# Last four k heads gathered by DMA from spare columns, and q/k products moved ahead of the attention phase

## The chip, the cores and the metric

One core of one Trainium2 chip. The metric is the device time of one launch in microseconds (us), median over runs; the profile's span is about 1.7 us shorter than the time. The three batches of experiments ran on three different chips, each beside the kernel before (medians 167.65, 167.1 and 167.67 us), so between batches compare ratios before medians.

## The reference

```python
# S=2048, D=448, H=16 heads of 28; window of 8 positions, dilation 2
xn  = layernorm(x)
qkv = (xn @ wqkv);  q, k, v = split into heads
logits = q . k[pos - 2*j] / sqrt(28),  j = 0..7, masked where pos - 2*j < 0
o   = softmax(logits) @ v[pos - 2*j]
s   = o @ wo
h   = gelu(xn @ w1 + b1) @ w2 + b2           # F = 1792
out = x + s * silu(h)
```

## The kernel before

Even and odd positions are put apart, so that the dilated window is 8 neighbours. A head has 28 columns and takes 32 partitions, so a tile of 128 holds four heads, and q and k need four tiles (g = 0..3) each. The four spare columns per head are unused. D = 448 is 3.5 blocks of 128 rows; two half blocks of 64 rows run side by side on TensorE. Work goes by chunks of 512 positions. In this text, phase 1, 2, 3 is the loop body for c = 0, 1, 2: a first FFN layer (`feed_forward_1`) and five attention units. A last FFN layer and two units follow. In a unit, S are the scores, E their exponentials (times a mask), psO the sums over the values, and o_t is an output tile on its way to DRAM.

```python
psA = tile_pool(bufs=2, PSUM);  psB = tile_pool(bufs=4, PSUM)   # psB is used in turn by all "B" tiles

def qk_pair(c, g, even, copies):        # q and k of 4 heads: 6 full matmuls + 2 of 64 rows
    ...
def v_job(b):                           # 4 matmuls of 448 columns, cast by ACT
    v_put(b, v_mm(b))
def wo_put(t, ps, cs=slice(0, D)):
    ...
    o_t = work.tile([P, D], BF16, name="o_t", tag="o_t", bufs=3)
    nc.vector.tensor_tensor(out=o_t[:, cs], in0=xt(t)[:, cs], in1=sg[:, cs], op=ALU.add)
    nc.sync.dma_start(dram_rows(out_par, t, 1)[:, 0, cs], o_t[:, cs])
def qk_unit(b, after_scores=lambda: None):   # 16 matmuls S = k.q ; exp on ACT ; mask on DVE
    ...
def av_unit(b, E):                           # 16 matmuls psO ; shuffle on DVE ; returns norm()
    ...
for c in range(3):
    feed_forward_1(c, ps, ...)          # with qk_pair(c + 1, 0) inside, output products behind k = 4
    n = c + 1
    qk_pair(n, 1, True, DD)
    for i in range(5):
        if i == 0:
            E = qk_unit(b, lambda: qk_pair(n, 2, ...))
            ...
            qk_pair(n, 3, True, DA)
        else:
            E = qk_unit(b); norm(); ffn2_job(4 * c + i - 1); v_job(next(vs))
            if n + 1 < NC:
                ln_apply(4 * n + 3 + i); ln_dma(4 * n + 3 + i)
        norm = av_unit(b, E)
    norm()
    ps = ffn1(n, 0, True)
```

The softmax here doesn't subtract the row's maximum and nothing guards it: scores larger than these inputs give would overflow.

## Time and profile before

| | before |
|---|---|
| time, median | 167.1 us |
| span of the profiled run | 165.6 us |
| TensorE busy | 158.9 us, 96% |
| VectorE, ACT busy | 68%, 76% |
| small copies on the queue of SyncE (wo) | 16, in 8.16 us |

The lines behind it are in the prediction. Names are PE for TensorE, DVE for VectorE, ACT for ScalarE, POOL for GpSimd, SP for SyncE and SPq for the queue on which SyncE issues DMAs. A timeline line gives start and duration in us, engine, source line, operation, what it writes and reads, and how many instructions are merged; the bracket is idle time before it and what ended it. TensorE has no gaps to speak of: a matmul removed is time removed, as long as nothing else falls behind.

### The profile page before, as it was taken

To read this page: it belongs to the slowest core of one execution; us is meant where nothing else is said; L and a number is where in the kernel's file an instruction comes from. 1 tells how busy PE (TensorE), PEld (TensorE's weight loads), DVE (VectorE), ACT (ScalarE), POOL (GpSimd) and SP (SyncE) were. 2 spreads that over 40 slices of the span, in tenths; PEclk is the share of its full clock that TensorE was granted. 3 is DMA by queue.
4 is the path that set the end of the run, shared out by engine and by line. 5 is a ranking of instruction groups with operands and counts; after the bars stand their busy time and mean duration, and the time that the engine had idled before them with its cause. 6 is when DMAs were issued, how large, how long until landed. Compare 5 with 4: busy or idle time off the path is not lost.

```text
span 165.6 us, 3242 instructions
## 1 busy us (share of the span) xinstructions
PE 158.9 (96%) x1290; PEld 71.8 (43%) x1301; DVE 112.9 (68%) x256; ACT 125.9 (76%) x198; POOL 4.5 (3%) x16
## 2 busy tenths in 40 slices
PE   6899999999999999999999999999999999999990
PEld 2343333345554334445554334335555334445570
DVE  5967890497888638687888308877777507678893
ACT  3773698598887795998887795698888698698830
POOL 7002000000000000000000000000000000000000
PEclk9999999999999999999999999999999999999999
DMA  5999995520111100100211100300000002020011
GB/s 134 302 306 267 325 190 93 164 44 4 32 36 32 32 0 4 55 0 0 36 32 32 36 0 0 112 1 4 0 4 0 0 0 60 31 83 0 4 55 55
DMA packets 15963, 10.62 MB, mean 64 GB/s; under 512 B 7500, under 2 KB 15948, under 8 KB 15948
## 3 DMA queue, kind: packets, MB, share of 16 engines
q1 hardware_dynamic: 15660, 10.18, 24.0%
q10 hardware_dynamic: 288, 0.23, 0.5%
q8 instruction: 10, 0.16, 0.4%
q14 instruction: 5, 0.04, 0.1%
HBM read 7.00 MB, written 1.84 MB: 53 GB/s over the span
## 4 chain that ended last, share of the span: by engine, by line
PE 83%; ACT 7%; DVE 5%; DMA 2%; issue 1%; DVEq 0%
PE ps_y L281 23%; PE ps_h L249 21%; PE ps_qk L197 11%; PE ps_v L228 8%; PE ps_s L331 6%; PE ps_h L258 4%; PE S L355 3%; PE psO L370 3%; ACT hT L264 3%; PE ps_qk L207 3%; DMA x<-in_A_x_dram 2%; ACT th L310 1%; DVE sg L337 1%; DVE st L161 1%; ACT L509 1%
## 5 line engine op out<-in xcount | busy, mean ns | idle before, releaser
L264 ACT ACTIVATE hT<-ps_h,b1f 128x512 bf16<-128x512 f32 x56 | 34.1, 695 | 10.1 <-PE ps_h L258 7.3
L249 PE MATMUL ps_h<-xnT,w 128*128 128x512 bf16 x161 | 39.3, 380 | 0.5 <-issue 0.2
L281 PE MATMUL ps_y<-w,hT 128*128 128x448 bf16 x196 | 39.5, 353 | 0.0
L361 ACT ACTIVATE E<-S 128x976 bf16<-128x976 f32 x34 | 31.6, 983 | 2.1 <-PE S L355 0.8
L281 PEld LDWEIGHTS <-hT 128*128 128x128 bf16 x196 | 18.0, 98 | 16.7
L249 PEld LDWEIGHTS <-w 128*128 128x128 bf16 x168 | 15.0, 98 | 22.1 <-issue 6.4
L363 DVE TENSOR_TENSOR E<-E,mk_gen 128x976 bf16<-128x976 bf16 x30 | 20.0, 666 | 6.7 <-ACT E L361 6.5
L197 PE MATMUL ps_qk<-xnT,wqk 128*128 128x512 bf16 x92 | 22.2, 380 | 0.3 <-issue 0.2
L379 DVE TENSOR_TENSOR oT<-psO,den 128x484 bf16<-128x484 f32 (+1 forms) x17 | 11.3, 662 | 10.1 <-ACT den L378 10.1
L214 DVE CAST qT<-ps_qk 128x512 bf16<-128x512 f32 x16 | 11.0, 687 | 9.5 <-PE ps_qk L207 8.4
L228 PE MATMUL ps_v<-wv,xnT 128*128 128x448 bf16 x68 | 15.7, 353 | 0.1
L311 DVE SCALAR_TENSOR_TENSOR g<-th,y 128x448 bf16<-128x448 bf16 x13 | 7.6, 621 | 10.8 <-ACT th L310 10.8
L337 DVE SCALAR_TENSOR_TENSOR sg<-ps_s,g 128x448 bf16<-128x448 f32 (+2 forms) x17 | 10.1, 592 | 7.0 <-PE ps_s L331 6.9
L233 ACT CAST vw<-ps_v 128x448 bf16<-128x448 f32 x17 | 9.1, 533 | 6.9 <-PE ps_v L228 6.8
L197 PEld LDWEIGHTS <-wqk 128*128 128x128 bf16 x96 | 8.9, 98 | 11.5 <-issue 1.8
L331 PE MATMUL ps_s<-wo,oT 128*128 128x448 bf16 (+2 forms) x68 | 13.4, 342 | 0.0
L377 ACT ACTIVATE den<-den 128x484 f32<-128x484 f32 (+1 forms) x17 | 10.3, 605 | 4.0 <-DVE den L374 4.0
L374 DVE STREAM_SHUFFLE den<-psO 128x484 f32<-128x484 f32 (+1 forms) x17 | 11.7, 695 | 0.0
L378 ACT ACTIVATE den<-den 128x484 f32<-128x484 f32 (+1 forms) x17 | 10.3, 606 | 0.5
L161 DVE BATCH_NORM_STATS2 st<-x 128x6 f32<-128x448 bf16 x16 | 9.8, 610 | 0.9 <-DMA x<-in_A_x_dram 0.8
L331 PEld LDWEIGHTS <-oT 128*128 128x128 bf16 x68 | 6.4, 98 | 5.9 <-issue 0.2
L228 PEld LDWEIGHTS <-xnT 128*128 128x128 bf16 x68 | 6.3, 98 | 6.0 <-ACT xnT L181 0.6
(71 smaller groups left out, 139.8 us busy)
## 6 DMA issues: line engine op xcount, KB each, us to landing
out_dram<-o_t SPq DMA_DIRECT2D x15, 112.0 KB
w<-in_B_w_dram SPq DMA_DIRECT2D x1, 1568.0 KB
x<-in_A_x_dram SPq DMA_DIRECT2D x3, 448.0 KB
w<-in_B_w_dram SPq DMA_DIRECT2D x2, 672.0 KB
wraw<-in_A_wqkv_dram SPq DMA_DIRECT2D x1, 672.0 KB
w<-in_B_w_dram SPq DMA_DIRECT2D x4, 112.0 KB
wo<-in_A_wo_dram SPq DMA_DIRECT2D x16, 24.5 KB
wv<-in_A_wqkv_dram SPq DMA_DIRECT2D x1, 336.0 KB
```

What stands on the lines that cost most here:

```text
L161: nc.vector.bn_stats(out=st[:], in_=xt(t))
L197: nc.tensor.matmul(ps[w][:, :], wqk[:, kt, 16 * w + 4 * g:16 * w + 4 * g + 4, :], xnT[:, kt, LEAD + c * CH:LEAD + (c + 1) * CH], start=(fi ...
L228: nc.tensor.matmul(ps[:, :], xnT[:, kt, o:o + P], wv[:, kt, :], start=(kt == 0), stop=(kt == KT - 1))
L249: nc.tensor.matmul(ps[i][:, :], w1[:, kt, m * P:(m + 1) * P], xnT[:, kt, LEAD + c * CH:LEAD + (c + 1) * CH], start=(first and kt == 0), st ...
L264: nc.scalar.activation(hT[:, m, :], ps[i][:, :], ACT.Gelu_apprx_tanh, bias=b1f[:, m:m + 1])
L281: nc.tensor.matmul(ps[:, :], hT[:, m, tt * P:(tt + 1) * P], w2[:, m, :], start=(m == 0), stop=(m == MT - 1))
L331: nc.tensor.matmul(ps[:, 0:n], oT[:, g, t * P:(t + 1) * P], wo[:, g, cs], start=(g == 0), stop=(g == 3))
L337: nc.vector.scalar_tensor_tensor(out=sg[:, cs], in0=ps[:, 0:cs.stop - cs.start], scalar=0.5, in1=g_sb[t % NG][:, cs], op0=ALU.mult, op1=AL ...
L361: nc.scalar.activation(ev, Sp[p2][:, :, :, 0:QW], ACT.Exp, scale=SCALE)
L363: nc.vector.tensor_tensor(out=ev, in0=ev, in1=mkb, op=ALU.mult)
L374: nc.vector.stream_shuffle(den[:, :, 0:n], psO[:, :, 0:n], [0] * 32)
L379: nc.vector.tensor_tensor(out=oT[:, :, QB * b:QB * b + n], in0=psO[:, :, 0:n], in1=den[:, :, 0:n], op=ALU.mult)
```

## The change

Intent: less work on TensorE. In chunks 1 to 3 the fourth tile of k is no longer a product of its own. Its 112 columns are spread over the spare columns of the other seven q and k tiles (four columns per 32), so that they come out of products made anyway, and 28 small copies per chunk (4 partitions of 1 KB each) bring them to their places in `kT`. q/k products go ahead of the attention units; the values of phases 2 and 3 are made in pairs in the first unit, so that their half blocks run side by side.

```diff
+    def qk_spare(kt):            # fills columns 28..31 of each slot with columns of the last 4 k heads
+        ...
+    def k3_rows(c, g, w):
+        j = 4 * w + g
+        cols = slice(LEAD + c * CH, LEAD + (c + 1) * CH)
+        for h in range(4):
+            nc.sync.dma_start(kT[32 * h + 4 * j:32 * h + 4 * j + 4, 3, cols],
+                              (qT, kT)[w][32 * h + DH:32 * h + 32, g, cols])
     def qk_put(c, g, w, ps, copies):
         copies[w]((qT, kT)[w][:, g, LEAD + c * CH:LEAD + (c + 1) * CH], ps[w][:, :])
+        if c:
+            k3_rows(c, g, w)
+    def q3_job(c, copy):         # q alone for g = 3: 4 matmuls
+        ...
+    def v_pair(b, copy=nc.scalar.copy):   # two value products, 6 full + 2 of 64 rows
+        ...
# feed_forward_1
-            if (c, k) in ((0, 6), (1, 4), (2, 4)):
-                qk_pair(c + 1, 0, True, DD)
+            if c in (1, 2) and k in (2, 3, 4):
+                qk_pair(c + 1, k - 2, False, DD)
+                if k == 3:
+                    q3_job(c + 1, nc.vector.tensor_copy)
-            if k in ((3, 5, 6) if c == 3 else (4,)):
+            if c == 3 and k in (2, 4, 6) or c in (1, 2) and k == 6:
                 ... wo_job
# first attention unit
-                    E = qk_unit(b, lambda: qk_pair(n, 2, False, ...))
+                if i == 0 and c == 0:
+                    E = qk_unit(b, lambda: q3_job(1, nc.vector.tensor_copy))
+                    ln_rstd(8, 4)
+                    qk_pair(1, 1, True, DA)
+                    qk_pair(1, 2, False, DA)
+                    nc.sync.dma_start(x_sb[3][:, :, :], dram_rows(x_par, 12, 4))
+                elif i == 0:
+                    E = qk_unit(b)
+                    if n + 1 < NC:
+                        ln_rstd(4 * n + 4, 4)
+                    v_pair(4 * n)
+                    v_pair(4 * n + 2, nc.vector.tensor_copy)
# later units
-                    v_job(next(vs))
+                    if c == 0 and i in (2, 4):
+                        v_pair(4 * n + i - 2)
```

Cut: start-up order, weight packing, `late_loads` moved behind the last layernorm transpose of phase 1, the order of two output products at the end.

## The prediction

> **What bounds the kernel now.** I read the page first, then the waits of TensorE, then the timeline of all engines around one attention phase, because the change moves work there.
>
> ```profile
> span 165.6 us, 3242 instructions
> ...
> PE 158.9 (96%) x1290; PEld 71.8 (43%) x1301; DVE 112.9 (68%) x256; ACT 125.9 (76%) x198; POOL 4.5 (3%) x16
> ...
> PE 83%; ACT 7%; DVE 5%; DMA 2%; issue 1%; DVEq 0%
> ```
>
> ```profile
> PE ps_w L389 <- DVE wz L98: 1.3, 1, 1.3
> PE pT L177 <- DVE xnb L169: 0.5, 2, 0.2
> ```
>
> TensorE is busy 96% of the span, makes 83% of the chain that ended last, and the waits over 0.2 us in its list (the second fence; us in total, times, longest) are 1.8 us at the start. So a matmul taken out shortens the kernel one for one, unless something then fails to keep up. The timeline of the second attention phase shows how near the others are. Columns are start, duration, instructions.
>
> ```profile
> 69.30 0.67 PE L355 MATMUL S<-qT,kT 28*128 28x122 bf16 x16
> 69.54 1.28 ACT L412 ACT_TABLE_LOAD   x1
> ...
> 77.94 0.40 PE L355 MATMUL S<-qT,kT 28*128 28x122 bf16 x16
> 78.27 2.82 PE L281 MATMUL ps_y<-w,hT 128*128 128x448 bf16 x14
> 78.38 1.86 ACT L361 ACTIVATE E<-S 128x976 bf16<-128x976 f32 x2
> ...
> 80.27 0.67 DVE L363 TENSOR_TENSOR E<-E,mk_gen 128x976 bf16<-128x976 bf16 x1 [0.16 <-ACT E L361]
> 80.76 0.61 ACT L378 ACTIVATE den<-den 128x484 f32<-128x484 f32 x1
> 80.93 0.92 PE L228 MATMUL ps_v<-wv,xnT 128*128 128x448 bf16 x4
> 81.40 0.67 DVE L379 TENSOR_TENSOR oT<-psO,den 128x484 bf16<-128x484 f32 x1 [0.46 <-ACT den L378]
> 81.78 0.40 PE L370 MATMUL psO<-E,vw 128*32 128x122 bf16 x16
> ```
>
> One attention unit is scores S, 14 products of the second FFN layer, 4 value products, then psO. The last mask product ends at 80.94, psO starts at 81.78: 0.84 us of slack, and the value products (0.85 us) are what gives it. Also S at 69.30 took 0.60 us to the next instruction (69.90), where 0.33 is usual: it waited for a late gelu. psO behind it lost 0.20. The same pair is seen in the third phase, so before already loses 2 x 0.47 = 0.94 us that no wait row names.
>
> **What the Trainium skill says.** TensorEngine Tiling (Array Packing), section Key Properties: changing the tiling mode drains TensorE. The trace agrees: 12 full matmuls of 512 columns run from 19.73 to 22.43 (2.70 us), 6 from 17.81 to 19.20 (1.39); six more cost 1.31, so 0.218 each, and 0.08 is left for the switch to 64-row matmuls. From the 448-column ones: 14 take 2.66 (0.190 each), 4 take 0.85 before a switch, leaving 0.09. I use 0.1 us per switch. Perfetto Trace Analysis, section Identifying the Most-Contended Engine, warns that matmul busy time is a poor measure. I therefore take start-to-start times, not the 380 ns mean durations, which overlap. DMA: Bandwidth & Descriptors, section Issuing engines are not separate DMA queues, says issuing costs the sequencer time and the engines are shared; here 16 loads of wo occupy the queue of SyncE from 27.30 for 8.16 us, 0.51 each (median duration 383 ns). Its section on the anatomy of one DMA gives about 2 us of fixed completion time, measured on another issue path; here an output buffer was writable again about 2.1 us after its store, so I use 2.
>
> **The change part by part.**
>
> *q/k products.* In chunks 1 to 3 the fourth pair (7 slots: 6 full and two 64-row matmuls side by side) becomes one q job of 4 full matmuls. 3 x 3 x 0.216 = 1.94 us less on TensorE.
>
> *Value pairs.* Six pairs take 7 slots of 448 columns in place of 8: 6 x 0.19 = 1.14 us less.
>
> *Switches.* Counting mode changes along each phase: the first attention phase gains 2 by its pairs and loses 1 by the missing q/k pair (+1); phases two and three have +2 each, since pairs no longer share borders so well; the last FFN phase puts output products behind k = 2 and 4 between 64-row groups that used to adjoin: +4. Together 9 x 0.1 = 0.9 us more. Net matmul saving 1.94 + 1.14 - 0.9 = **2.2 us**.
>
> *Removed stalls.* The 0.94 us above go away in that form, as the FFN phases get more TensorE work (q/k) for the same gelus.
>
> *Start.* A bias transpose leaves the border before the first q/k pair and weight copies come in fewer instructions: 0.1 us gained. One more warm-up matmul may give it back.
>
> *New stall: units without value products.* In phases two and three units 1 to 4 are S, 14 products, psO: 4.17 - 0.76 = 3.42 us. Counting from the end E of S (78.34): exponentials until E+1.9; logarithm and exponential of the former unit until E+3.03 (80.76+0.61 = 81.37); VectorE takes oT at E+3.06, y at 3.64, the two layernorm instructions at 4.17, shuffle at 4.69, the next unit's two masks from 5.29 to 6.76 (they took 1.47 together at 83.63). psO's tail and the next S need 0.38 + 0.40: so two units cannot take less than 7.54 us where TensorE wants 6.86. Units 2 and 4 of phase two each lose 0.68: 1.36 us. Phase three has no layernorm there; the same chain without its 0.52 gives 7.02, 0.16 over: with its second occurrence 0.25 us. Phase one keeps a value pair in units 2 and 4; unit 3 starts behind their two ACT copies: 0.1 us.
>
> *New stall: first unit of phase two.* Only two output products (1.6 us) stand between the last FFN tile and S. From that tile's end K (67.58 before): gelu until K+1.96, table until K+3.26, exponentials until about K+5.0, then two small layernorm instructions (0.44) and the first value copy (0.54): K+6.05. psO takes the PSUM slot of that first value tile (four slots, the fifth allocation), so it cannot start earlier. TensorE would be there at K+1.62 + 0.7 for a waiting S + 3.06 for the pairs = K+5.4. Loss 0.65 on psO and 0.37 on S: 1.0 us. In phase three four output products stand there, enough to hide it.
>
> *Row gathers.* 84 small DMAs on SyncE, 28 per chunk: 28 x 0.47 = 13.2 us of issuing per chunk (my estimate between 383 and 510 ns). In phase one they start at about 31.2 and land by 46.4; unit 4, the first to read them, comes at about 47.6. Mean loss 0.3 us. In phase three they hold the output stores back on the in-order queue until some 20.3 us into the phase, and the fourth output tile of that phase needs the buffer of the first (three buffers), so VectorE could be blocked ahead of the masks: up to 1 us, 0.6 taken.
>
> *VectorE and ACT.* About 8 casts (chunk copies and value copies, 0.55 to 0.69 us) move from ACT to VectorE, five tiny copies of spare columns are new (an estimate of 0.2 us each). They lie in FFN phases where VectorE was idle for up to 4.5 us at a time.
>
> *End.* An output product moves ahead of a biased FFN tile: same TensorE sum, no change assumed.
>
> Sum: 167.07 - 2.2 - 0.94 - 0.1 + (1.36 + 0.25 + 0.1) + 1.0 + 0.3 + 0.6 = 167.1. I choose **166.6**, half a microsecond lower, because the worst-case terms (DMA 0.9) were taken generously and the arrangement looks tuned for these very waits.
>
> **Rivals.**
> - *All of the saving arrives* (no new stalls): 167.07 - 2.2 - 0.94 - 0.1 = 163.8, hardly 2%. For it: TensorE is the bound and nothing waits for long today. Against: the slack of 0.84 us in a unit is the value products themselves.
> - *VectorE becomes the bound of units 1 to 4*: its work per unit there is 3.57 us against 3.42 on TensorE. That is in my sum as the chain of 7.54; if its instructions slow by 0.2 us more per unit, 8 units give +1.6: 168.2.
> - *The gathers are late*: 28 x 0.6 us of issuing would make unit 4 of phase one wait about 3 us and block phase three about 2: 170 or a little over. Against: descriptors are few and each load of wo, with more rows, issued in 0.51.
> - *They are hidden wholly*, being off the path with 15 us to spare: 165.7 to 166.
>
> **Range and chances.** The terms that may fail are the stalls (3 us in total, each perhaps half as large) and the DMAs (0 to 4). So 164.7 to 168.7. Faster by over 2% needs below 163.73, all new stalls absent: 0.08. Slower by over 2% needs above 170.4, the late gathers: 0.06. Within 2%: 0.86.
>
> **What would show it.** Matmul starts of TensorE: 9 full and 6 value slots fewer. In phase two the start-to-start of units alternates 3.4 and 4.1 us; psO of its first unit waits for the ACT copy of the first value tile. VectorE shows no idle time between psO units there. Busy of TensorE falls by about 2 to 3 us, its waits for E or vw rise. Wrong if TensorE stays without gaps in phases two and three (then near 164), or if S of unit 4 or the masks stand behind a DMA (then slower).

## The result

175.8 us median (175.48 to 175.97, 4 runs) against 167.1: the ratio is 1.0504 (95% interval 1.0466 to 1.0543), slower by 5%. Ratios are the mean time of one kernel's fast runs over that of the other's of the same rounds, so not quite the ratio of the medians quoted. 175.8 lies far outside the range of 164.7 to 168.7.

The page of the changed kernel, with the rows of TensorE busy and of its granted clock in 40 slices. A digit is tenths.

```profile
span 174.2 us, 3345 instructions
...
PE 161.5 (93%) x1281; PEld 71.9 (41%) x1290; DVE 116.1 (67%) x263; ACT 121.5 (70%) x190; POOL 4.5 (3%) x16
...
PE   7999999999979999998999999990999999999991
...
PEclk9999999999978999999999999999699999999998
```

TensorE has fewer matmuls and yet a longer busy time: its clock is below full in two places, each next to a hole in the first row (47.9 and 117.6 us; the 8 in the last slice is the end of the run). The list of waits (us in total, times, longest) names both holes; before, it had no row of this kind.

```profile
DVE o_t L381 <- DMA out_dram<-o_t: 4.5, 1, 4.5
...
PE psO L411 <- DVE E L404: 4.4, 3, 3.9
...
PE S L396 <- DMA kT<-kT: 1.6, 4, 0.5
```

**Phase 1, unit 4.** The timeline of TensorE. Ahead of it the queue of SyncE issues the gathers of chunk 1 from 30.63 to 48.5.

```profile
47.15 0.34 PE L396 MATMUL S<-qT,kT 28*128 28x122 bf16 x12
47.86 0.22 PE L396 MATMUL S<-qT,kT 28*128 28x122 bf16 x1 [0.37 <-DMA kT<-kT]
...
49.23 0.21 PE L396 MATMUL S<-qT,kT 28*128 28x122 bf16 x1 [0.51 <-DMA kT<-kT]
49.79 0.21 PE L396 MATMUL S<-qT,kT 28*128 28x122 bf16 x1 [0.35 <-DMA kT<-kT]
49.93 4.51 PE L324 MATMUL ps_y<-w,hT 128*128 128x448 bf16 x14
```

```profile
30.63 2.65 SPq L208 DMA_DIRECT2D kT<-qT  x4
...
46.09 2.44 SPq L208 DMA_DIRECT2D kT<-kT  x4
```

The last four scores (at 47.86, 48.50, 49.23, 49.79) come about 0.64 us apart, which is the pace of the gathers (28 of them from 30.63 to the next entry of the queue at 48.58: 0.64 each). S takes from 47.15 to 49.93, 2.78 us where 0.33 is usual: 2.45 us lost. Then the 14 products of the second FFN layer take 4.34 us to the next instruction (54.27) where 2.66 is usual: another 1.68, at half clock. A stretch of the profile (its end points, its length, busy time of PE, PEld, DVE, ACT and POOL, then granted clock, busy share of the DMA engines and GB/s) shows the half; the same view of the time of the gathers shows DMA engines that are nearly idle, so it is not the transfers that are slow:

```profile
31.00:48.00 17.00, 16.62 (x194) 7.90 (x193) 13.33 (x28) 13.68 (x21) 0.00 (x0) 1.00 0.03 9
51.00:53.00 2.00, 2.00 (x7) 0.84 (x6) 1.33 (x2) 1.12 (x3) 0.00 (x0) 0.50 0.98 240
```

**Phase 3, first unit.** The gathers of chunk 3 fill the queue from 100.83 to 118.69, and four output stores of the same phase stand behind them.

```profile
113.20 0.39 DVE L381 TENSOR_TENSOR o_t<-x,sg 128x448 bf16<-128x448 bf16 x1
...
118.69 2.61 SPq L382 DMA_DIRECT2D out_dram<-o_t  x4
120.54 0.39 DVE L381 TENSOR_TENSOR o_t<-x,sg 128x448 bf16<-128x448 bf16 x1 [4.49 <-DMA out_dram<-o_t]
120.85 1.24 DVE L404 TENSOR_TENSOR E<-E,mk_gen 128x976 bf16<-128x976 bf16 x2
121.57 0.23 PE L411 MATMUL psO<-E,vw 128*32 128x122 bf16 x2 [3.85 <-DVE E L404]
122.14 0.59 PE L411 MATMUL psO<-E,vw 128*32 128x122 bf16 x14 [0.34 <-DVE E L404]
...
123.19 3.96 PE L324 MATMUL ps_y<-w,hT 128*128 128x448 bf16 x14
```

The first of the four output tiles was ready at 113.59; its store was issued at 118.69. The fourth needs its buffer, so VectorE waited 4.49 us with the masks behind it. psO, which TensorE could have begun at 117.65 (the value pair ahead of it starts its last two products at 117.35, and these take 0.30 elsewhere), ran its main part from 122.14: 4.5 us later. Both psO and the S behind it then ran slowly, so that the 14 products began at 123.19. Between 117.65 and 123.19 lie 5.54 us where e1 below needs 0.69: 4.85 us lost. Another 1.23 were lost in the 14 products, which took 3.89 us (to 127.08).

The ledger: the prediction had 0.3 for the first and 0.6 for the second place. Measured over predicted is (2.45 - 0.3) + 1.68 + (4.85 - 0.6) + 1.23 = 9.3 us; 9.2 lie between 166.6 and 175.8. The match is closer than it deserves: the prediction's own terms add up to 167.44, not to 167.1 or 166.6, so some 0.9 us of errors in its other terms cancel. So the claim to test is that two waits on one queue, with the clock that they cost, are the whole of the error.

### The profile page after: what moved, and what is told of

It reads as the page before. It is cut to its first block, busy times and chain, and to the rows that moved or that the text cites. A ratio compares the mean times of both kernels' runs of the same rounds, so it can differ in the third digit from the quotient of the medians.

```text
span 174.2 us, 3345 instructions
## 1 busy us (share of the span) xinstructions
PE 161.5 (93%) x1281; PEld 71.9 (41%) x1290; DVE 116.1 (67%) x263; ACT 121.5 (70%) x190; POOL 4.5 (3%) x16
## 4 chain that ended last, share of the span: by engine, by line
PE 72%; ACT 11%; DVE 8%; SPq 3%; issue 2%; DMA 2%; DVEq 0%
PE ps_h L292 20%; PE ps_y L324 19%; PE ps_qk L214 10%; PE ps_h L301 4%; ACT E L402 3%; SPq L208 3%; PE ps_w L430 3%; PE ps_s L372 3%; PE psO L411 3%; PE S L396 3%; PE ps_v L257 2%; ACT hT L307 2%; DVE sg L378 2%; PE ps_qk L224 2%; DVE E L404 1%
## 5 line engine op out<-in xcount | busy, mean ns | idle before, releaser
L324 PE MATMUL ps_y<-w,hT 128*128 128x448 bf16 x196 | 42.3, 371 | 0.0
L324 PEld LDWEIGHTS <-hT 128*128 128x128 bf16 x196 | 18.9, 102 | 18.8 <-issue 3.5
L404 DVE TENSOR_TENSOR E<-E,mk_gen 128x976 bf16<-128x976 bf16 x30 | 19.5, 665 | 6.8 <-ACT E L402 6.8
L234 DVE CAST qT<-ps_qk 128x512 bf16<-128x512 f32 x16 | 10.9, 686 | 17.9 <-PE ps_qk L214 14.6
L214 PE MATMUL ps_qk<-xnT,wqk 128*128 128x512 bf16 x77 | 18.9, 380 | 0.0
L411 PE MATMUL psO<-E,vw 128*32 128x122 bf16 x272 | 7.7, 224 | 5.0 <-DVE E L404 4.4
L214 PEld LDWEIGHTS <-wqk 128*128 128x128 bf16 x78 | 6.7, 97 | 10.8 <-issue 4.2
L262 ACT CAST vw<-ps_v 128x448 bf16<-128x448 f32 x13 | 6.5, 540 | 5.4 <-PE ps_v L277 4.7
L347 DVE TENSOR_TENSOR y<-ps_y,b2bc 128x448 f32<-128x448 f32 x14 | 8.6, 617 | 2.0 <-PE ps_y L324 2.0
L396 PE MATMUL S<-qT,kT 28*128 28x122 bf16 x272 | 8.1, 220 | 1.8 <-DMA kT<-kT 1.6
```

Of the source, the lines that this page charges most:

```text
L214: nc.tensor.matmul(ps[w][:, :], wqk[:, kt, 16 * w + 4 * g:16 * w + 4 * g + 4, :], xnT[:, kt, LEAD + c * CH:LEAD + (c + 1) * CH], start=(fi ...
L324: nc.tensor.matmul(ps[:, :], hT[:, m, tt * P:(tt + 1) * P], w2[:, m, :], start=(m == 0), stop=(m == MT - 1))
L396: nc.tensor.matmul(Sp[h // 2][:, h % 2, g, 0:QW], kT[r, g, o - 7:o - 7 + P], qT[r, g, o:o + QW], start=True, stop=True)
L404: nc.vector.tensor_tensor(out=ev, in0=ev, in1=mkb, op=ALU.mult)
L411: nc.tensor.matmul(psO[32 * h:32 * h + 32, g, 0:QW], vw[:, b, 4 * g + h, :], E[:, h, g, 0:QW], start=True, stop=True)
```

## The experiments

Theories. **Queue**: gathers take so long to issue on SyncE that unit 4 waits for rows and VectorE for an output buffer; each gap also drops TensorE's clock. Rivals: the units are late by their own chains (masks, casts, value copies) and the DMA only goes along; the transfers, not their issue, are slow; the slow products behind the gaps come from memory traffic.

### Five output buffers: e1_ot5

```diff
-    o_t = work.tile([P, D], BF16, name="o_t", tag="o_t", bufs=3)
+    o_t = work.tile([P, D], BF16, name="o_t", tag="o_t", bufs=5)
```

> The changed kernel with five output buffers (o_t) in place of three. Theory (VectorE is blocked ahead of the masks of the third phase's first unit, because the fourth output tile needs the buffer of the first, whose store stands behind 28 gathers on SyncE): the 3.85 + 0.34 us gap before psO goes, and with it the slow clock after it (14 products took 3.89 us where 2.66 is usual): 175.8 - 5.2 = about 170.6 us. Rival (psO of that unit is late by its own chain of exponentials, masks and value copies): gap and time stay, about 175.8.

169.65 us median (168.2 to 169.87), ratio to before 1.0109. The timeline of TensorE at the same place:

```profile
117.34 0.43 PE L411 MATMUL psO<-E,vw 128*32 128x122 bf16 x16
117.70 0.40 PE L396 MATMUL S<-qT,kT 28*128 28x122 bf16 x16
118.03 2.82 PE L324 MATMUL ps_y<-w,hT 128*128 128x448 bf16 x14
```

The gap is gone and the products behind it run at full clock. The stores are as late as before; only the buffer was missing. The saving of 6.1 us is 0.9 more than I wrote, because I had counted the waits of psO (3.85 + 0.34) and not the whole delay (4.85; with the slow products 4.85 + 1.23 = 6.1). Of the four runs, three took 169.6 to 169.9 at a mean clock of 0.990, one 168.2 at 0.996: the drop of clock in phase 1 does not come in full in every run.

### Chunk 1 without gathers: e2_full1

```diff
-        if c:
+        if c > 1:
             k3_rows(c, g, w)
-                    E = qk_unit(b, lambda: q3_job(1, nc.vector.tensor_copy))
+                    E = qk_unit(b, lambda: qk_pair(1, 3, False, DD))
```

> The changed kernel, but chunk 1 takes its fourth k heads by a full q/k pair, with no gathers for that chunk. Theory (issuing 28 gathers at 0.635 us each makes S of unit 4 of the first phase wait 2.45 us, and the clock it loses costs 1.68 us in the 14 products behind it): 2.45 + 1.68 - 3 matmuls of 0.216 = 3.5 us less, about 172.3. Rival (those scores wait for something that the gathers only accompany, such as late casts of q and k): the wait stays, 175.8 + 0.65 = about 176.4.

173.45 us (172.87 to 174.21), ratio 1.0357. S of unit 4 takes 0.33 us again (47.90 to 48.23) and the products behind it 2.65; the gap of phase 3 is still there. The saving is 2.4 us, 1.1 less than expected. Part of that is scatter of the clock: two runs at a mean clock of 0.987 took 172.9 and 173.1 us, two at 0.98 took 173.8 and 174.2. The latter lost as much clock as the change with its two gaps; where they lost it is not known, as neither was profiled.

### Both: e3_both

The two edits above together.

> Both edits at once. Theory: the two stalls are independent, so the savings add: 175.8 - 5.2 - 3.5 = about 167.1 us, level with the kernel before. Rival (removing one stall only exposes another, as the queue of SyncE is full throughout): 169 or more.

167.07 us (166.93 to 167.09), ratio 0.9971. As expected: the savings add (6.1 + 2.4 = 8.5 of the 8.7 seen), so the two stalls are independent, and without them the changed kernel stands level with the one before. No run of it has a mean clock under 0.997: with the gaps, the loss of clock goes too.

### Dummy matmuls in the gap: e4_warm

```diff
                     v_pair(4 * n + 2, nc.vector.tensor_copy)
+                    if c == 2:
+                        busy(17)
```

> The changed kernel with 17 dummy matmuls of 512 columns put into the 3.85 us gap before psO in the third phase's first unit: they do no useful work and the gap stays as long. Theory (TensorE's clock falls to half after a gap of this length, and the 14 products behind it pay for that): the 14 products take 2.66 us again in place of 3.89, 1.2 us less, about 174.6. Rival (these products are slow because of PSUM or memory traffic piled up behind the stall): no change or slower, 175.8 or more.

174.35 us (172.68 to 174.57), ratio 1.0387. VectorE is blocked for 4.5 us as before, psO is as late, but now:

```profile
115.91 3.84 PE L430 MATMUL ps_w<-wz 128*128 128x512 bf16 x17
119.84 0.23 PE L411 MATMUL psO<-E,vw 128*32 128x122 bf16 x2
120.41 0.39 PE L411 MATMUL psO<-E,vw 128*32 128x122 bf16 x14 [0.35 <-DVE E L404]
...
121.06 2.82 PE L324 MATMUL ps_y<-w,hT 128*128 128x448 bf16 x14
```

The products take their usual 2.66 us behind the same wait on the same data. This profiled run also kept the full clock behind the gap of phase 1, where no dummies stand, so it shows what the clock does and not what the dummies do. There the 14 products take 2.66 us (49.89 to 52.55) against 4.34 in the change, with as much DMA traffic beside them (the same view as above, clock 1.00 in place of 0.50):

```profile
51.00:53.00 2.00, 2.00 (x13) 1.05 (x11) 1.53 (x3) 1.08 (x2) 0.00 (x0) 1.00 1.06 244
```

In the change the slow products of phase 3 ran without any DMA traffic (123.2 to 125.2, share 0.00). So the rival of memory traffic falls: it is TensorE's clock. What the dummies do is read from the other three runs. The Trainium skill describes this in TensorE: Matmul & The Clock Gate, section Part 1: The HAM clock gate: a monitor halves the clock after an idle window of about 3.4 us, and the window is free-running. The trace agrees on the half (granted clock 0.50 from 51.0 to 53.0 and from 123.2 to 125.2 in the changed kernel), and a free-running window would fit it that the drop comes in some runs only: the profiled one is the fastest of its four (172.68, clock 1.000), the other three took 174.3 to 174.6 at 0.99. That leaves room for one drop, where the four runs of the change (0.977 to 0.980) have two; as e1, with the gap of phase 1 alone, is at 0.99 in three of four too, I take the drop that is gone for that of phase 3. No profile of a slower run shows it.

### No gathers at all: e5_nogather

```diff
-        if c:
-            k3_rows(c, g, w)
-                    E = qk_unit(b, lambda: q3_job(1, nc.vector.tensor_copy))
+                    E = qk_unit(b, lambda: qk_pair(1, 3, False, DD))
-                    q3_job(c + 1, nc.vector.tensor_copy)
+                    qk_pair(c + 1, 3, True, DD)
```

> The changed kernel without any gathers: all chunks take their fourth k heads by a full q/k pair at the place of the q job; the rest of the rearrangement (q/k products ahead, value pairs, output products moved) stays. Theory: both stalls and their slow clock go (9.4 us), 9 matmuls of 0.216 come back: 175.8 - 9.4 + 1.9 = about 168.3 us, so the rearrangement alone costs about a microsecond over the kernel before. Rival (the rearrangement is worth its value pairs, 1.1 us, and more): 166 or less.

168.63 us (168.56 to 168.75), ratio 1.0090. The rearrangement without its main saving costs 1.5 us over the kernel before. I read this as value pairs that do not pay for the switches of mode and for the waits in phase 2 (the pairs were not tested alone). These waits are all still in this trace (psO waits 0.55 for a value copy, units of 3.4, 3.9 and 3.6 us).

### Half of chunk 1's gathers on GpSimd: e6_split

```diff
-            nc.sync.dma_start(kT[32 * h + 4 * j: ...
+            (nc.sync, nc.gpsimd)[h % 2 if c == 1 else 0].dma_start(kT[32 * h + 4 * j: ...
```
with five output buffers.

> The changed kernel with five output buffers, and for chunk 1 every second gather issued by GpSimd in place of SyncE. Theory (the issuing queue is the limit, not the transfer): SyncE is done 7 to 8 us earlier, S of unit 4 does not wait if GpSimd keeps up with 14 issues in some 15 us: 175.8 - 5.2 - 4.1 = about 166.5 us, slightly under the kernel before. Rival (the transfers themselves or their landing are slow, whoever issues): S still waits, about 170.6.

166.99 us (166.91 to 167.03), ratio 0.9989. Both queues had issued all 28 by 39.9, in place of 48.5, and the list of TensorE's waits is empty around unit 4. Two queues halve the transfers of each as well as the issues; but the DMA engines were busy 3% while the change issued its gathers, and GpSimd moves the same bytes in more packets (448 for its 14 gathers, 32 each, against 8 each from SyncE), so it is the issue, not the transfer. S of unit 4 still takes 0.85 us where 0.33 is usual, with no wait shown; what that is was not tested. It is about as much as the time lies above what I expected.

```profile
38.13 1.03 POOL L208 DMA_DIRECT2D kT<-kT  x2
38.69 1.21 SPq L208 DMA_DIRECT2D kT<-kT  x2
47.23 0.92 PE L396 MATMUL S<-qT,kT 28*128 28x122 bf16 x16
48.08 2.82 PE L324 MATMUL ps_y<-w,hT 128*128 128x448 bf16 x14
```

### All gathers on GpSimd: e7_pool

```diff
-            nc.sync.dma_start(kT[32 * h + 4 * j: ...
+            nc.gpsimd.dma_start(kT[32 * h + 4 * j: ...
```
with three output buffers, as in the change.

> The changed kernel with three output buffers as it is, all 84 gathers issued by GpSimd. Theory: output stores are no longer behind gathers, so the third phase's gap goes; the first phase depends on the pace of GpSimd: at under 0.5 us each about 166.5, at 1 us each unit 4 of the first phase waits some 10 us, about 177. Rival (the blocked output buffer is not due to the shared queue): the third phase's gap of 3.85 us stays in either case.

166.27 us (166.19 to 166.55), ratio 0.9949. One word changed in the kernel, and 9.5 us are back. The timeline of GpSimd:

```profile
30.88 2.19 POOL L208 DMA_DIRECT2D kT<-qT  x4 [18.18 <-DVE qT L234]
33.05 2.05 POOL L208 DMA_DIRECT2D kT<-kT  x4
...
43.60 2.05 POOL L208 DMA_DIRECT2D kT<-kT  x4
```

GpSimd, idle until then, issues four in 2.05 us (0.51 each, against 0.635), done at 45.65, and S of unit 4 (at 47.12) has no wait; it takes 0.56 us, against 0.33 as usual and 2.78 in the change. The wait for an output buffer shrinks from 4.5 to 0.3 us with the same three buffers, so the shared queue was its cause.

### What an issue costs: e8_probe

The kernel before with 24 copies that nothing reads, at idle times of the queue of SyncE.

```diff
+            for j in range(4):
+                nc.sync.dma_start(d[4 * j:4 * j + 4, :], wz[4 * j:4 * j + 4, :])               # 4 rows, on chip
+            for j in range(4):
+                nc.sync.dma_start(d[32 + 16 * j:48 + 16 * j, :], wz[32 + 16 * j:48 + 16 * j, :])   # 16 rows
+            for j in range(4):
+                nc.sync.dma_start(d[96 + 4 * j:100 + 4 * j, 0:D], A_wo[4 * j:4 * j + 4, :])     # 4 rows, DRAM
+            ...                                                                              # 128, 28, 8 rows, on chip
```

> The kernel before with 24 probe copies on SyncE at times when its queue is idle, in six groups of four: between parts of on-chip memory with 4, 16, 128, 28 and 8 rows, and from DRAM with 4 rows. It asks what makes a gather take 0.577 us to issue where a store takes 0.333. Theory (the number of rows[...]): 4 and 8 rows take about 0.58 wherever they come from, 16 and 128 rows 0.33 to 0.44, 28 rows between. Rival (the on-chip source): all five on-chip groups take about 0.58, and the 4 rows from DRAM 0.33 to 0.44. Time stays at 167.

The timeline of the queue, in the order 4, 16, 4 from DRAM, then (behind two stores) 128, 28 and 8 rows:

```profile
55.68 2.62 SPq L147 DMA_DIRECT2D pr<-wz  x4
58.35 2.44 SPq L149 DMA_DIRECT2D pr<-wz  x4
60.84 1.48 SPq L151 DMA_DIRECT2D pr<-in_A_wo_dram  x4
...
67.57 2.47 SPq L154 DMA_DIRECT2D pr<-wz  x4
70.08 3.30 SPq L156 DMA_DIRECT2D pr<-wz  x4
73.43 3.14 SPq L158 DMA_DIRECT2D pr<-wz  x4
```

Medians are 0.597, 0.584, 0.293, 0.596, 0.774 and 0.642 us. My theory of row counts is wrong: 4, 16 and 128 rows cost the same. The rival holds: a copy that reads on-chip memory and writes it takes about twice as long to issue as one that reads DRAM, with a smaller effect for 28 and 8 rows. Those two groups also have the shortest rows (64 bytes, against 1 KB for 4 and 16 rows and 128 bytes for 128), so which of the two it is stays open. Whether the source or the pair of both ends counts, these groups do not tell.

### A version that beats both: e9_pool_ot5 to e12_lnearly

Each adds one edit to the one above it; five rounds on one chip, the kernel before at 167.67 there.

```diff
# e9_pool_ot5: gathers on nc.gpsimd and o_t with bufs=5
# e10_c3: the last FFN phase as in the kernel before
-            if c == 3 and k in (2, 4, 6) or c in (1, 2) and k == 6:
+            if c == 3 and k in (3, 5, 6) or c in (1, 2) and k == 6:
#         and silu behind k = 3 and 5
# e11_rstd: first unit of phases 2 and 3
                     E = qk_unit(b)
-                    if n + 1 < NC:
-                        ln_rstd(4 * n + 4, 4)
                     v_pair(4 * n)
                     v_pair(4 * n + 2, nc.vector.tensor_copy)
+                    if n + 1 < NC:
+                        ln_rstd(4 * n + 4, 4)
# e12_lnearly: units 1 to 4
                     E = qk_unit(b)
+                    if n + 1 < NC:
+                        ln_apply(4 * n + 3 + i); ln_dma(4 * n + 3 + i)
                     norm()
#         and no longer behind the value products
```

> The changed kernel with all gathers issued by GpSimd and five output buffers. Theory: what is left of the wait for an output buffer (0.3 us on VectorE) and of the waiting psO in the third phase goes, about 166.0 us. Rival: that wait lies off the path already, 166.3 as with three buffers.

> The same, and the last FFN phase as in the kernel before: output products and silu behind k = 3, 5 and 6. Theory (a change of tiling mode costs TensorE about 0.1 us, and this arrangement saves four): 0.4 us less, about 165.6. Rival (the changed order was put there to spare VectorE or ACT a wait, which comes back): no gain or slower.

> The same, and in the first unit of phase two the two small layernorm instructions on ACT come behind the value copies. Theory (psO there waits for the ACT copy of the first value tile because it takes its PSUM slot): 0.44 us of the 0.55 us wait goes, about 165.2. Rival (psO is held as long by the masks): no gain.

> The same, and in units 1 to 4 the layernorm instructions come ahead of the former unit's normalization on VectorE, where it idles 0.46 us for ACT. Theory (two units cannot be shorter than a chain of 7.54 us because VectorE takes these 0.52 us behind oT): the chain shrinks to 7.1 us, and of about 1 us lost in phase two 0.6 to 0.8 comes back, about 164.5. Rival (units there are held by VectorE's sum of work, 3.57 us, whatever the order): 0.3 us at most.

| | median us | range | ratio to before | 95% interval |
|---|---|---|---|---|
| e9_pool_ot5 | 166.27 | 166.11 to 166.62 | 0.9932 | 0.9911 to 0.9952 |
| e10_c3 | 165.87 | 165.65 to 166.19 | 0.9904 | 0.9883 to 0.9924 |
| e11_rstd | 165.71 | 165.52 to 165.94 | 0.9894 | 0.9874 to 0.9913 |
| e12_lnearly | 164.94 | 164.76 to 165.24 | 0.9850 | 0.9826 to 0.9875 |

e9 is e7 within the scatter: with the queue free, a third buffer suffices. e10 gives the 0.4 us that four switches of mode were put at, though it moves other work too and its range touches that of e9. e11 gives 0.16, not 0.44, which is within the scatter; the next lines suggest why. e12 gives 0.77, as expected of the chain. Its timeline of TensorE in phase 2, first unit to third:

```profile
74.80 0.67 PE L411 MATMUL psO<-E,vw 128*32 128x122 bf16 x16
75.41 0.39 PE L396 MATMUL S<-qT,kT 28*128 28x122 bf16 x16
...
78.81 0.40 PE L396 MATMUL S<-qT,kT 28*128 28x122 bf16 x16
...
82.23 0.44 PE L396 MATMUL S<-qT,kT 28*128 28x122 bf16 x16
...
85.69 0.40 PE L396 MATMUL S<-qT,kT 28*128 28x122 bf16 x16
```

Units are 3.40, 3.42 and 3.46 us apart where the change had 3.41, 3.87 and 3.65: the layernorm instructions fit into the time in which VectorE waited for ACT. psO at 74.80 now takes 0.61 us to the next S in place of 0.34; I read that as the masks holding it instead of the value copy, which would be why e11 gained little, but no run took the masks' part away. e12 is 1.5% faster than the kernel before.

## Why the prediction was wrong

Its mechanisms were right. One number, the issue time of a gather, mis-sized two terms of its sum by a factor of eight, and one effect was missing. Besides, the sum is added wrongly: its terms give 167.44, not 167.1, so 166.6 lies 0.84 below them and not 0.5.

- **Failed: the row gathers, "28 x 0.47 = 13.2 us of issuing per chunk".** I took 0.47 us from the loads of wo, which read DRAM, and below even their pace of 0.51. The on-chip gathers went at 0.635 us each, 17.9 us per chunk with the gaps between groups (30.63 to 48.58); e8 shows that it is their kind. In phase 1 "Mean loss 0.3 us" was 2.45. The estimate had 1.2 us in hand before unit 4; 28 x 0.165 = 4.6 us more issuing used it up, and I should have asked what the error of a factor multiplied by 28 is.
- **Failed: the output buffer, "up to 1 us, 0.6 taken".** The chain as told (gathers ahead of stores, three buffers, VectorE blocked ahead of the masks) is what the trace shows, and e1 and e7 confirm it from both ends. Its size was 4.85 us, and the same 0.47 is behind it. An estimate from the trace: 28 issues of 0.47 from 100.83 would have let the first store go at 114.0, and the buffer be free at about 115.9 (1.85 us from issue to the waiting write, 118.69 to 120.54), before VectorE wanted it at 116.05. So 0.6 was ample for 0.47. The 2.1 us that the prediction reads for this from the kernel before is an upper bound only: no write waited for a buffer there.
- **Missing: the clock.** Nothing in the prediction priced what a gap does to TensorE afterwards: 1.68 + 1.23 us (e4).
- **Right: the rival "The gathers are late".** It named this course with 0.6 us of issuing per gather and "170 or a little over"; at 0.635, and without the clock, it fell short by some 5 us. It had been given 0.06. "Each load of wo, with more rows, issued in 0.51" was my ground against it, and e8 shows that rows are not what counts.
- **Right: new waits in phase 2.** First unit: 1.0 predicted, 0.37 on S and 0.55 on psO measured, together 0.92. Units 1 to 4: 1.36 predicted; starts 79.50, 82.91, 86.78, 90.43 and about 94.1 give 0.96 over 3.42 each. e12 confirms the chain. The alternation of 3.4 and 4.1 was not as sharp.
- **Right: the saving on TensorE is small and paid back.** With both stalls out of the way (e7, e9) the change is 0.5 to 0.7% faster than before, 166.3 us. The prediction's terms without its 0.9 us for the DMAs add up to 166.5, and with 1.94 us of q/k products put back to 168.5, where e5 took 168.6. Lowering the sum to 166.6 had no ground in the end. The single terms were not all measured; e10 agrees with 0.1 us for a switch.
- **Undecided.** The start gained 0.38 us (first FFN matmul at 17.43, not 17.81) where I had 0.1; which of its edits did it was not tested.

## What to carry to other kernels

Copies that are tiny in bytes can be the largest user of an issuing queue: count them, multiply by the issue time of that kind of copy (same source, same issuer), and look at what stands behind them on the same in-order queue, above all stores whose buffers an engine needs back. If another engine is idle, let it issue them. Here a gap on TensorE cost its own length (2.45 and 4.85 us) and, in most runs, another 1.68 and 1.23 us in slow clock.

## What the Trainium skill lacked or had wrong

- DMA: Bandwidth & Descriptors, section Issuing engines are not separate DMA queues, calls the issue time usually small relative to the DMA itself. That may hold for one gather; what it leaves out is that issues add up on one queue. Here this decided the result: 28 gathers of 4 KB at 0.635 us each held the queue for 17.9 us while the DMA engines were busy 3%, and moving all 84 to GpSimd gave 9.5 us.
- No page that I read gives the issue time by kind of source: about 0.58 to 0.60 us for on-chip to on-chip copies of 4, 16 and 128 rows on SyncE, 0.293 for 4 rows from DRAM.
- The same page, section Issuing engine by pattern, has the sync and scalar path as generally faster than that of GpSimd. For these copies GpSimd was the faster issuer, 0.51 us against 0.635.
- TensorE: Matmul & The Clock Gate puts the drop of clock behind an idle window of about 3.4 us; for a stretch broken by matmuls it gives no figure. Here a stretch of 2.8 us that held 16 short matmuls was followed by half clock in two profiled runs (the change and e1) and not in a third (e4).
